# Local and global attention with a squared-ReLU MLP on one core: the jobs of the global rows, the block output copies and the weight decoding at other places of the step, and VectorE and ScalarE in program order from the first step

## The chip, the core and the metric

The kernel runs on one core of a Trainium2 chip. The metric is the device time of one execution in microseconds (us). Three runs of the kernel before gave 1134.98, 1136.09 and 1137.07 us, so the median is 1136.09 us. One more execution was profiled; it is the source of all the rows below.

In the rows, PE is TensorE's matmuls and PEld its weight loads, DVE is VectorE, ACT is ScalarE and SP is SyncE, whose queue issues every DMA of this kernel.

## The reference

Eight batches of eight heads, 512 local and 32 global positions, head dimension 64. Each local position attends to the 32 global keys and to the local keys within 32 positions; each global position attends to all 544 keys. The 4352 output rows then go through a two-layer MLP with hidden size 2048. The shape of the MLP's input is 4352 x 512.

```python
k_all = np.concatenate([k_g, k_l], axis=2)
s_g = scale * np.matmul(q_g, k_all.transpose(0, 1, 3, 2))
out_g = np.matmul(sm(s_g), v_all)
s_ll = np.where(np.abs(pos[:, None] - pos[None, :]) <= 32, scale * q_l @ k_l.T, -1e9)
a_l = sm(np.concatenate([s_lg, s_ll], axis=-1))
out_l = np.matmul(a_l, np.concatenate([v_g, v_l], axis=2))
x = np.concatenate([out_g, out_l], axis=2).transpose(0, 2, 1, 3).reshape(B * S, H * D)
h = np.maximum(x @ w_in, 0.0)
return h * h @ w_out
```

## The kernel before

**Steps.** One loop over t from 0 to 145 does everything. In step t the attention works on local head t: there are NT = 128 of them, each one head of one half batch (256 queries). In the same step the MLP works on m = t - 9: eight consecutive m are the eight slices of the hidden layer for one block of 256 rows, and there are 17 blocks, the last one made of all the global rows. So `gemm1(m)` (input times a slice of w_in, into the PSUM tile h, one buffer) and `gemm2(m-1)` (the squared slice times w_out, accumulated over eight steps into the two PSUM tiles o) are in every step from 9 on, and a step is named by its t. Work on attention has an eight step rhythm, and global work a rhythm of sixteen, one batch.

**A step's order.** For TensorE: in odd steps `av` (probabilities times values of two heads into the first half of the PSUM tile xa), then jobs, then `transposes(t-1)`, the scores of head t+1 (`begin`), `gemm1(m)`, `gemm2(m-1)`. For VectorE and ScalarE: in odd steps `x_evac` (ScalarE copies xa to x_h, VectorE then reads xa and x_h to write x_l), `pt_evac(t-1)` (each copies half of the transposed probabilities, pts), `softmax3(t)` (VectorE: add, reciprocal, two scalings), `split_head(t+2)` (ScalarE hi, VectorE lo), `softmax1(t+1)` (VectorE: mask and maximum, into st), `softmax2(t+1)` (ScalarE: two exponentials with their sums), the copies and additions of the global score rows (sg), `act1(m)` (ScalarE ReLU from h to r, VectorE r = h * r) and `act2(m)` (ScalarE gh, VectorE gl). For the first 16 heads, and for block 0 of the MLP, the matmuls are plain float32 and hi, lo, gh and gl fall away; block 0 squares on ScalarE.

**Jobs of the global rows.** Twice per batch, four heads' worth of global rows are ready. `g_soft` (VectorE maximum over 544 scores), `g_exp` (ScalarE exponential), `g_norm` (VectorE reciprocal), `g_load_v` (DMA), `g_tr` (ten transposes), `g_evac` (gp), `g_av` (ten matmuls into the second half of xa), `g_xs` (ScalarE copy of xa, gxs) and `g_x` (eight VectorE 32x32 transposes into xg) are hung on steps and on places within them: lines 598 to 612.

**Block outputs.** `evac(blk)` copies the two o tiles on ScalarE into ot tiles, which DMAs then store. It stands in the steps with m % 8 == 1, ahead of that step's `gemm2`, which starts the next block in the same o tiles.

**Weights.** 32 chunks of 512 KB each hold float64 weights. A chunk is loaded (wr), decoded by one ScalarE operation (`w_abs`, into wf) and two VectorE passes (`w_bits`, a letter b in PLAN each), and for the blocks after the first it is split into ws (a letter s: one ScalarE cast and one VectorE subtraction). PLAN[t] has four places per step, divided by commas: after `rise`, after the jobs "soft", after `act2`, and at the step's end. LOOK says how many chunks are loaded ahead of the one in decoding; `w_need` decodes what is missing at the start of a step.

**What sets the order.** A scheduler orders instructions, except where `InOrder` marks them to be kept in program order. FREE holds the first step from which VectorE, ScalarE and TensorE are so marked. The SP queue isn't marked; it issues in the order in which its rows stand, and a row waits there for its buffer: raw (a head's queries and keys) has 4, v 7, the weights 32 in all.

Of the kernel before, what the change touches and what calls it, by code (L numbers as in the profile page):

```python
# [7 lines left out]
F32 = mybir.dt.float32  # L8
# [8 lines left out]
P = 128  # L17
# [8 lines left out]
NSTEP = NBLK * 8  # L26
# [2 lines left out]
SCALE = 0.125  # L29
CHUNKS = ((0, 128), (320, 128), (128, 96), (224, 96))  # L30

PLAN = [",,,b", "b,,,b", "b,,,b", "b,,b,", "b,,b,", "b,,b,", "b,,b,", "b,b,,b", "b,b,,b", "bb,bb,bb,bb", "bb,bb,bb,bb", "bbs,bb,bbs,bbs", "bbs,bbs,bbs,bbs", "bbs,bbs,bbs,bbs", "bbs,bbs,bs,s", "ss,s,s,s", "ss,s,s,s", "s,,s,", "s,,s,", "s,,s,", "s,,s,", "s,,s,", "s,,s,"]
FREE = (17, 17, 0)
LOOK = 2
SQ = (0, 8)
WCH = 32

# [1 line left out]
def f(ap):  # L39
    return ap.bitcast(F32)  # L40
# [19 lines left out]
def attention_moe(  # L60
# [10 lines left out]
    nc = tc.nc  # L71
# [4 lines left out]
    p2 = ctx.enter_context(tc.tile_pool(name="p2", bufs=2))  # L76
# [15 lines left out]
    def w_take(n):  # L92
        w_bufs["free"] -= n

    def load_head(t):
        raw = pq.tile([P, QK], F32, tag="raw", name=f"raw{t}")
        v = pv.tile([P, VC], F32, tag="v", name=f"v{t}")
        nc.sync.dma_start(raw, qk[t])
        nc.sync.dma_start(v, vv[t])
        heads[t] = dict(raw=raw, v=v)  # L100

    load_head(0)
    con = cp.tile([P, P + 4 * WIN], F32, name="con")
    for o, e in ((0, P + 2 * WIN), (P + 2 * WIN, P + 4 * WIN)):
        nc.sync.dma_start(con[:, o:e], consts[:, o:e])
# [79 lines left out]
    def g_add(t):  # L185
        if plain(t):
            return
        for dst, src in g_parts(t):
            ve.tensor_add(dst, src[:32], dst)
# [39 lines left out]
    def transposes(t):  # L229
        pr = prob[t % 2]  # L230
        for i, (o, n) in enumerate(CHUNKS):
            for u in range(2):
                r = half(u)
                pe.transpose(pt[u][:n, 64 * i : 64 * i + 64], pr[r, o : o + n], ident[r, r])
# [7 lines left out]
    def av(t):  # L242
        pair = [heads[t], heads[t + 1]]
        for i in range(3):
            for e, hd in enumerate(pair):
                v, pts, o = hd["v"], hd["pts"], xa[half(e), :HALF]
                if i == 0:
                    pe.matmul(o, v[:96, 128:192], pts[:96, 2:4, :], start=True, stop=False, skip_group_check=True)
                else:
                    u = i - 1  # L250
                    pe.matmul(
                        o[:, P * u : P * u + P],
                        v[:, half(u)],
                        pts[:, u, :],
                        start=False,
                        stop=i == 2,
                        skip_group_check=True,
                    )

    def x_evac(t):  # L260
        g, c = t // 8, (t % 8) // 2
        x = xa[:, :HALF]
        if g == 0:
            ac.copy(xg[:, c, :], x)
        else:
            ac.copy(x_h[:, g % 2, c, :], x)
            ve.tensor_sub(x_l[:, g % 2, c, :], x, f(x_h[:, g % 2, c, :]))
        heads[t] = heads[t + 1] = None

    state = {}  # L270

    def g_load(t):

        b, grp = t // 16, (t // 4) % 2
        qr = p2.tile([P, P], F32, tag="qr", name=f"qr{t}")
        nc.sync.dma_start(qr, qg[b, grp])
        state["q", t // 4] = qr

    def g_split(t):
        if plain(t):  # L280
# [144 lines left out]
    def act2(m):  # L425
        r = moe["r"]
        if m < 8:
            moe["g", m] = (r,)
            return
        gh = p2.tile([P, 2, HALF], F32R, tag="gh", name=f"gh{m}")  # L430
        gl = p2.tile([P, 2, HALF], F32R, tag="gl", name=f"gl{m}")
        ac.copy(gh, r)
        ve.tensor_sub(gl, r, f(gh))
        moe["g", m] = (gh, gl)
# [23 lines left out]
    def evac(blk, tiles=(0, 1)):  # L458
        for i in tiles:
            ot = p2.tile([P, DM], F32, tag="ot", name=f"ot{blk}_{i}")  # L460
            ac.copy(ot, moe["o"][i])
            if blk < NGR:
                b, hf = divmod(blk, 2)
                r0 = b * 544 + 32 + hf * 256 + i * P
                nc.sync.dma_start(out[r0 : r0 + P, :], ot)
            else:
                for bb in range(4):
                    r0 = (4 * i + bb) * 544
                    nc.sync.dma_start(out[r0 : r0 + 32, :], ot[32 * bb : 32 * bb + 32, :])
# [4 lines left out]
    def w_start(i):  # L474
        while w_next["load"] < min(WCH, i + LOOK) and w_bufs["free"] >= 2:
            w_take(1)
            w_load(w_next["load"])
            w_next["load"] += 1
        if i < w_next["load"] and i not in w_ready and (i % 2 == 1 or w_bufs["free"] >= 1):
            w_ready.add(i)  # L480
            w_abs(i)
# [29 lines left out]
    def w_tick(t, place):  # L511
        if t < len(PLAN):
            for c in PLAN[t].split(",")[place]:
                {"b": w_pass, "s": w_chunk}[c]()

    def w_need(m):

        if m < 8:
            while w_next["bits"] < 8 * m + 8:
                n = w_next["bits"]  # L520
                w_pass()
                assert w_next["bits"] > n
        elif m < 16:
            while not set(range(4 * (m - 8), 4 * (m - 8) + 4)) <= whi.keys():
                n = w_next["split"]
                w_chunk()
                assert w_next["split"] > n, (m, w_next, w_bufs, sorted(w_used)[-1:])
# [6 lines left out]
    def run_jobs(t, place):  # L534
        for job, *args in jobs.pop((t, place), ()):
            job(*args)

    def begin(t):
        scores(t)
        g_scores(t)  # L540

    def rise(t):
        softmax1(t)
        softmax2(t)

    g_load(0)
    w_start(0)
    begin(0)
    rise(0)
# [2 lines left out]
    for t in range(NSTEP + LAG + 1):  # L552
        m = t - LAG
        ve.on, ac.on, pe.on = [t >= x for x in FREE]
        prev, run, live, more = 1 <= t <= NT, 0 <= m < NSTEP, t < NT, t + 1 < NT
        pair = t - 3 if t % 2 and 3 <= t <= NT + 1 else None
        if t + 4 < NT:
            load_head(t + 4)
        if t % 4 == 0 and t + 4 < NT:
            g_load(t + 4)  # L560
        if run:
            w_need(m)

        if pair is not None:
            av(pair)
            x_evac(pair)
        run_jobs(t, "av")
        run_jobs(t, "tr")
        if prev:
            transposes(t - 1)  # L570
        if more:
            begin(t + 1)
        if run:
            gemm1(m, 0)
            gemm1(m, 1)
        if prev:
            pt_evac(t - 1)
        run_jobs(t, "evac")
        if live:
            softmax3(t)  # L580
        if t + 2 < NT:
            split_head(t + 2)
        if more:
            rise(t + 1)
        if 0 < m <= NSTEP and m % 8 == 1 and m > 8:
            evac(m // 8 - 1)
        w_tick(t, 0)
        if more:
            g_copy(t + 1)
            g_add(t + 1)  # L590
        run_jobs(t, "soft")
        if t % 4 == 2 and t + 2 < NT:
            g_split(t + 2)
        w_tick(t, 1)
        if run:
            act1(m)
        run_jobs(t, "late")
        if live and t % 4 == 3 and (t // 8) % 2 == 1:
            d = t if t % 8 == 3 else t + 1
            e = d + 4 if d % 2 else d + 5  # L600
            for at, place, job in (
                (d + 1, "soft", g_soft),
                (d + 1, "soft", g_exp),
                (d + 2, "soft", g_norm),
                (d + 2, "late", g_load_v),
                (d + 3, "tr", g_tr),
                (d + 3, "evac", g_evac),
                (e, "av", g_av),
                (e, "evac", g_xs),
                (max(e, 17), "late", g_x),  # L610
            ):
                jobs.setdefault((at, place), []).append((job, t))
        if m == NSTEP:
            for i in range(2):
                gemm2(m - 1, 0, (i,))
                gemm2(m - 1, 1, (i,))
                evac(NBLK - 1, (i,))
        elif m > 0:
            gemm2(m - 1, 0)
            gemm2(m - 1, 1)  # L620
        if run:
            act2(m)
        w_tick(t, 2)
        if 0 < m <= 8:
            w_done(m - 1)
        w_tick(t, 3)
        if 8 * NGR - 2 <= m < 8 * NGR:
            cols = (slice(0, 224), slice(224, HALF))[m % 2]
            ac.copy(x_h[:, 0, :, cols], xg[:, :, cols])
            ve.tensor_sub(x_l[:, 0, :, cols], xg[:, :, cols], f(x_h[:, 0, :, cols]))  # L630
# [69 lines left out]
```

## Time and profile before

| | |
|---|---|
| median of three runs | 1136.09 us |
| the profiled execution, its own time | 1137.75 us |
| its span, first to last instruction | 1135.9 us |
| mean granted TensorE clock | 0.972 |
| VectorE busy, ScalarE busy | 669.6 us, 552.6 us |
| loaded from HBM, stored | 65.54 MB, 8.91 MB |

The busy shares of the engines and the chain of work that ended last are quoted with the prediction. The profile divides the span in 40 slices of 28.4 us. In the first two TensorE is at 5 and 8 tenths and VectorE at 5 and 8; from the seventh to the 36th TensorE is at 8 or 9 tenths, VectorE at 5 or 6 and ScalarE at 4 or 5. The granted TensorE clock is at 7 tenths of full speed in the second slice, 8 in the fourth and sixth, and 9 or more in all others. The DMA engines are busy to 8 tenths in the first three slices and to 1 or 2 tenths after.

### The profile page before, as it was taken

To read this page: it belongs to the slowest core of one execution; us is meant where nothing else is said; L and a number is where in the kernel's file an instruction comes from. 1 tells how busy PE (TensorE), PEld (TensorE's weight loads), DVE (VectorE), ACT (ScalarE), POOL (GpSimd) and SP (SyncE) were. 2 spreads that over 40 slices of the span, in tenths; PEclk is the share of its full clock that TensorE was granted. 3 is DMA by queue.
4 is the path that set the end of the run, shared out by engine and by line. 5 is a ranking of instruction groups with operands and counts; after the bars stand their busy time and mean duration, and the time that the engine had idled before them with its cause. 6 is when DMAs were issued, how large, how long until landed. Compare 5 with 4: busy or idle time off the path is not lost.

```text
span 1135.9 us, 21870 instructions
## 1 busy us (share of the span) xinstructions
PE 1052.2 (93%) x8320; PEld 878.9 (77%) x8320; DVE 669.6 (59%) x2340; ACT 552.6 (49%) x1617; POOL 0.5 (0%) x5
## 2 busy tenths in 40 slices
PE   5898799998999989998999989998999989999998
PEld 4665578877888778877888778877888778878987
DVE  5886466565666556655666656656566666663321
ACT  5786445545554445544455454545454454543222
POOL 0000000000000000000000000000000000000000
PEclk9798989999999999999999999999999999999999
DMA  8881111121211212121211212112211212101000
GB/s 267 275 298 52 32 58 48 52 62 57 61 56 40 62 53 62 59 59 48 66 42 53 62 52 62 58 53 61 57 45 56 58 53 66 43 1 43 1 20 19
DMA packets 72458, 75.88 MB, mean 67 GB/s; under 512 B 6304, under 2 KB 63776, under 8 KB 72352
## 3 DMA queue, kind: packets, MB, share of 16 engines
q1 hardware_dynamic: 72352, 74.47, 21.6%
q8 instruction: 66, 1.08, 0.4%
q14 instruction: 40, 0.33, 0.1%
HBM read 65.54 MB, written 8.91 MB: 66 GB/s over the span
## 4 chain that ended last, share of the span: by engine, by line
PE 53%; DVE 23%; ACT 14%; issue 4%; DMA 4%; SPq 0%; ACTq 0%; DVEq 0%
PE o L53 22%; PE h L53 19%; PE xa L53 6%; DVE prob L53 6%; ACT prob L53 5%; PE sb L53 3%; DVE gl L53 3%; DVE r L53 3%; ACT gh L53 2%; PE pt L53 2%; DVE st L53 2%; DVE lo L53 2%; ACT r L53 2%; ACT sg L53 2%; DMA wr<-in_w_dram 2%
## 5 line engine op out<-in xcount | busy, mean ns | idle before, releaser
L53 PE MATMUL h<-x_h,ws 128*128 128x256 f32 x2048 | 400.8, 289 | 6.1 <-DVE r L53 6.1
L53 PE MATMUL o<-ws,gh 128*128 128x512 f32 x1024 | 326.2, 400 | 25.7 <-ACT ot L53 25.7
L53 PEld LDWEIGHTS h<-x_h,ws 128*128 128x128 f32 x2048 | 327.6, 191 | 22.0 <-DVE r L53 7.5
L53 PE MATMUL h<-x_l,ws 128*128 128x256 f32 x1024 | 289.9, 283 | 0.1
L53 ACT ACTIVATE prob<-prob,st 128x224 f32<-128x224 f32 x256 | 121.3, 475 | 259.9 <-DVE st L53 259.7
L53 PEld LDWEIGHTS o<-ws,gh 128*128 128x128 f32 x1024 | 187.0, 192 | 62.2 <-ACT ot L53 29.3
L53 PE MATMUL o<-ws,gl 128*128 128x512 f32 x512 | 203.5, 398 | 0.0
L53 PEld LDWEIGHTS h<-x_l,ws 128*128 128x128 f32 x1024 | 196.1, 192 | 1.0 <-DVE x_l L53 0.4
L53 DVE TENSOR_TENSOR sg<-sb,sg 32x128 f32<-32x128 f32 (+3 forms) x280 | 60.1, 257 | 159.5 <-ACT sg L53 159.3
L53 DVE TENSOR_TENSOR r<-h,r 128x512 f32<-128x512 f32 x128 | 88.4, 691 | 104.2 <-ACT r L53 104.0
L53 DVE TENSOR_TENSOR gl<-r,gh 128x512 fp32r<-128x512 f32 x128 | 88.7, 693 | 77.3 <-ACT gh L53 76.8
L53 ACT CAST gh<-r 128x512 fp32r<-128x512 f32 x128 | 79.3, 619 | 97.5 <-DVE r L53 97.5
L53 PEld LDWEIGHTS o<-ws,gl 128*128 128x128 f32 x512 | 97.7, 191 | 22.9
L53 ACT ACTIVATE r<-h 128x512 f32<-128x512 f32 x136 | 81.3, 598 | 61.1 <-PE h L53 58.1
L53 DVE CUSTOM_DVE_ANT_0 prob<-sb,con 128x224 f32<-128x224 f32 x248 | 86.4, 386 | 9.4 <-PE sb L53 9.1
L53 DVE COPY pts<-pt 128x256 f32<-128x256 f32 x128 | 53.5, 418 | 40.5 <-PE pt L53 40.0
L53 DVE TENSOR_SCALAR prob<-prob,st 128x224 f32<-128x224 f32 x256 | 74.7, 334 | 4.2
L53 ACT COPY pts<-pt 128x256 f32<-128x256 f32 x128 | 47.5, 371 | 60.0 <-PE pt L53 59.0
L53 PEld LDWEIGHTS xa<-pts,v 128*64 128x64 f32 (+1 forms) x768 | 47.5, 141 | 35.8 <-issue 24.1
L53 PEld LDWEIGHTS pt<-con,prob 64*128 64x128 f32 (+1 forms) x1024 | 42.3, 137 | 41.5 <-issue 27.5
L53 PE MATMUL xa<-pts,v 128*64 128x128 f32 (+1 forms) x768 | 73.9, 327 | 0.2 <-ACT pts L53 0.2
L53 PE MATMUL pt<-con,prob 64*128 64x64 f32 (+1 forms) x1024 | 61.7, 242 | 8.0 <-DVE prob L53 7.9
(69 smaller groups left out, 1050.4 us busy)
## 6 DMA issues: line engine op xcount, KB each, us to landing
raw<-in_qk_dram SPq DMA_DIRECT2D x128, 176.0 KB, 2.3
wr<-in_w_dram SPq DMA_DIRECT2D x32, 512.0 KB, 5.5
v<-in_vv_dram SPq DMA_DIRECT2D x128, 96.0 KB, 1.9
gv<-in_vg_dram SPq DMA_DIRECT2D x32, 320.0 KB, 3.4
out_dram<-ot SPq DMA_DIRECT2D x32, 256.0 KB, 2.0
qr<-in_qg_dram SPq DMA_DIRECT2D x32, 64.0 KB, 2.3
out_dram<-ot SPq DMA_DIRECT2D x8, 64.0 KB, 1.7
con<-in_consts_dram SPq DMA_DIRECT2D x1, 288.0 KB, 4.3
```

Of the source, the lines that this page charges most:

```text
L53: r = method(*args, **kwargs)
```

## The change

It does six things. `evac` goes from behind `rise` to the very front of its step. `g_av` and `g_xs` go from steps 15 and 21 of a batch's sixteen to steps 16 and 20, so from odd to even ones. `g_soft`, `g_exp`, `g_norm` and `g_x` go from their places ahead of `act1` or behind it to a new place "post", behind `act2`. FREE is 0 for all three engines, so the first 17 steps are in program order on VectorE and ScalarE too. PLAN has one decoding pass in each of steps 0 to 7 (two or three before, and one in step 0), four in step 8 (three before) and eight in each of steps 9 to 14 (the same before in steps 9 to 13, where the scheduler moved them besides); the splits end two steps later. LOOK is 4. The first load of global queries stands ahead of the constants in SP's queue.

```diff
-PLAN = [",,,b", "b,,,b", "b,,,b", "b,,b,", "b,,b,", "b,,b,", "b,,b,", "b,b,,b", "b,b,,b", "bb,bb,bb,bb", "bb,bb,bb,bb", "bbs,bb,bbs,bbs", "bbs,bbs,bbs,bbs", "bbs,bbs,bbs,bbs", "bbs,bbs,bs,s", "ss,s,s,s", "ss,s,s,s", "s,,s,", "s,,s,", "s,,s,", "s,,s,", "s,,s,", "s,,s,"]
-FREE = (17, 17, 0)
-LOOK = 2
+PLAN = [",,,b", ",,,b", ",,,b", ",,,b", ",,,b", ",,,b", ",,,b", ",,,b", "b,b,b,b", "b,bb,bbb,bb", "b,bb,bbb,bb", "b,bb,bbbs,bbs", "b,bb,bbbs,bbs", "bs,bb,bbbs,bbs", "bs,bb,bbbs,bbs", "b,bb,bbss,bs", "s,s,s,", "s,,s,s", "s,,s,s", "s,,s,", "s,,s,", "s,,s,", "s,,s,", "s,,s,"]
+FREE = (0, 0, 0)
+LOOK = 4
...
     load_head(0)
+    g_load(0)
     con = cp.tile([P, P + 4 * WIN], F32, name="con")
...
-    g_load(0)
     w_start(0)
...
         if run:
             w_need(m)
 
+        if m > 8 and m % 8 == 1:
+            evac(m // 8 - 1)
         if pair is not None:
             av(pair)
...
-        if 0 < m <= NSTEP and m % 8 == 1 and m > 8:
-            evac(m // 8 - 1)
...
-            e = d + 4 if d % 2 else d + 5
+            e = d + 5 if d % 2 else d + 4
             for at, place, job in (
-                (d + 1, "soft", g_soft),
-                (d + 1, "soft", g_exp),
-                (d + 2, "soft", g_norm),
+                (d + 1, "post", g_soft),
+                (d + 1, "post", g_exp),
+                (d + 2, "post", g_norm),
                 (d + 2, "late", g_load_v),
                 (d + 3, "tr", g_tr),
                 (d + 3, "evac", g_evac),
                 (e, "av", g_av),
                 (e, "evac", g_xs),
-                (max(e, 17), "late", g_x),
+                (max(e, 17), "post", g_x),
...
         if run:
             act2(m)
+        run_jobs(t, "post")
         w_tick(t, 2)
```

Three places show the moves. The first is TensorE's queue around a `g_av` of the second batch, before the change (step 31). xa is the tile that `av` and `g_av` share, gv and gp are the values and probabilities of the global rows, pt takes the transposes.

```order
L53 MATMUL o_2_2166<-ws_1092,gl_2474 128x512
L53 MATMUL xa<-pts_2430,v_1896 64x256
L53 MATMUL xa<-pts_2534,v_1987 64x256
L53 MATMUL xa<-pts_2430,v_1896 64x128
L53 MATMUL xa<-pts_2534,v_1987 64x128
L53 MATMUL xa<-pts_2430,v_1896 64x128
L53 MATMUL xa<-pts_2534,v_1987 64x128
L53 MATMUL xa<-gv_2458,gp_2537 64x128 x10
L53 MATMUL pt_112<-con,prob_108 128x64
```

The same `g_av` in the changed kernel (step 32), on the same engine:

```order
L53 MATMUL o_2_2165<-ws_1477,gh_2580 128x512 x2
L53 MATMUL o_2_2165<-ws_1477,gl_2581 128x512
L53 MATMUL o_2_2166<-ws_1477,gh_2580 128x512 x2
L53 MATMUL o_2_2166<-ws_1477,gl_2581 128x512
L53 MATMUL xa<-gv_2456,gp_2537 64x128 x10
L53 MATMUL pt_114<-con,prob_111 128x64
```

The ten matmuls stood right behind an `av` into the same tile; now there is no `av` in their step, and they follow the step's last `gemm2`.

The second place is ScalarE's queue in steps 33 and 34, before the change: from a global exponential (sg, gst) over the block copies (ot) to the next ReLU (r).

```order
L53 ACTIVATE sg,gst_2864<-sg,gst_2864 128x544
L53 ACTIVATE r_2868<-h_2818 128x512
L53 CAST gh_2883<-r_2868 128x512
L53 COPY pts_2934<-pt_112 128x4x64
L53 CAST hi_2941<-raw_2699 128x352
L53 ACTIVATE prob_109,st_2945<-prob_109,st_2945 128x224 x2
L53 COPY ot_0_2951<-o_2_2165 128x512
L53 COPY ot_1_2954<-o_2_2166 128x512
L53 COPY sg<-sb_110 32x128
L53 COPY sg<-sb_111 32x160
L53 CAST qz_2963<-qr_2703 128x4x32
L53 ACTIVATE r_2966<-h_2909 128x512
```

The same stretch of ScalarE's queue in the changed kernel:

```order
L53 ACTIVATE r_2864<-h_2818 128x512
L53 CAST gh_2879<-r_2864 128x512
L53 ACTIVATE sg,gst_2883<-sg,gst_2883 128x544
L53 COPY ot_0_2891<-o_2_2165 128x512
L53 COPY ot_1_2894<-o_2_2166 128x512
L53 COPY pts_2940<-pt_114 128x4x64
L53 CAST hi_2947<-raw_2679 128x352
L53 ACTIVATE prob_111,st_2951<-prob_111,st_2951 128x224 x2
L53 COPY sg<-sb_112 32x128
L53 COPY sg<-sb_113 32x160
L53 CAST qz_2961<-qr_2683 128x4x32
L53 ACTIVATE r_2964<-h_2915 128x512
```

The block copies stood between the exponentials of a head and its sg copies, and now stand ahead of pts; the global exponential stood ahead of a ReLU, and now stands behind gh.

The third place is VectorE's queue at the first two heads, before the change. prob_108 and st_130 belong to head 0, prob_109 and st_154 to head 1; ISA rows are `softmax1`, and wf is weight decoding.

```order
L53 TENSOR_SCALAR st_130<-st_130 128x2
L53 ISA prob_109,st_154<-s_0_144,con 128x224
L53 ISA st_154 128x1
L53 ISA prob_109,st_154<-s_1_145,con 128x224
L53 ISA st_154 128x1
L53 TENSOR_SCALAR wf_124<-wf_124 128x512
L53 TENSOR_SCALAR st_154<-st_154 128x2
L53 SCALAR_TENSOR_TENSOR wf_124<-wr_120,wf_124 128x512
L53 TENSOR_SCALAR st_130<-st_130 128x2
L53 RECIPROCAL st_130<-st_130 128x2
L53 TENSOR_SCALAR prob_108<-prob_108,st_130 128x224 x2
```

VectorE at the same place in the changed kernel, where head 0 is prob_110 and head 1 is prob_111:

```order
L53 TENSOR_SCALAR st_134<-st_134 128x2 x2
L53 RECIPROCAL st_134<-st_134 128x2
L53 TENSOR_SCALAR prob_110<-prob_110,st_134 128x224 x2
L53 ISA prob_111,st_158<-s_0_148,con 128x224
L53 ISA st_158 128x1
L53 ISA prob_111,st_158<-s_1_149,con 128x224
L53 ISA st_158 128x1
L53 TENSOR_SCALAR st_158<-st_158 128x2
L53 TENSOR_SCALAR wf_128<-wf_128 128x512
```

`softmax1` of head 1 stood ahead of `softmax3` of head 0, and now stands behind it; this holds for every following pair of heads.

More of the change, by code (lines that the diff above doesn't have):

```diff
@@ L100, in load_head, with g_load @@
         heads[t] = dict(raw=raw, v=v)
+    state = {}
+    def g_load(t):
+        b, grp = t // 16, (t // 4) % 2
+        qr = p2.tile([P, P], F32, tag="qr", name=f"qr{t}")
+        nc.sync.dma_start(qr, qg[b, grp])
+        state["q", t // 4] = qr
     load_head(0)
+    g_load(0)
     con = cp.tile([P, P + 4 * WIN], F32, name="con")
@@ L268, in x_evac @@
         heads[t] = heads[t + 1] = None
[L270 to L277, printed above, removed]
     def g_split(t):
```

## The prediction

> **What bounds the kernel now.** I read the page's busy times first, then its chain, then TensorE's waits behind the early part, then the rhythm of the chain, and last the rows of one step.
>
> ```profile
> PE 1052.2 (93%) x8320; PEld 878.9 (77%) x8320; DVE 669.6 (59%) x2340; ACT 552.6 (49%) x1617; POOL 0.5 (0%) x5
> ...
> PE 53%; DVE 23%; ACT 14%; issue 4%; DMA 4%; SPq 0%; ACTq 0%; DVEq 0%
> ```
>
> TensorE is busy for 93%, yet only 53% of the chain is TensorE's, and 37% is VectorE's and ScalarE's, which are busy 59% and 49% of the time. So a second chain, in which these two engines wait for each other, is nearly as long as TensorE's work. TensorE's waits from 148 us to the end:
>
> ```profile
> PE xa L53 <- DVE x_l L53: 23.1, 14, 2.3
> PE o L53 <- ACT ot L53: 20.8, 13, 2.3
> PE h L53 <- DVE r L53: 5.0, 6, 0.8
> ```
>
> Two waits, once per eight steps each, make up nearly all: `g_av` waits for `x_l`, `gemm2` for the block copies. Now the rhythm, from the chain (each row is a step's `gemm1`):
>
> ```profile
> 246.28 3.07 PE h L53 x24
> ...
> 304.12 3.07 PE h L53 x24
> ...
> 311.89 3.07 PE h L53 x24
> 318.65 3.07 PE h L53 x24
> ...
> 764.93 3.22 PE h L53 x24
> ```
>
> 246.28 is step 31 and 764.93 step 95: four periods of sixteen steps, (764.93 - 246.28) / 4 = 129.66 us each. Without a wait, a step into an odd one takes 7.77 us (304.12 to 311.89), one into an even one 6.76. Eight of each are 116.2. What else TensorE has in a period is in its timeline:
>
> ```profile
> 233.56 0.46 PE L53 MATMUL pt<-con,sg 64*128 64x64 f32 x8
> ...
> 240.69 1.09 PE L53 MATMUL xa<-pts,v 96*64 96x256 f32 x12
> 244.06 1.31 PE L53 MATMUL xa<-gv,gp 128*64 128x128 f32 x20 [2.28 <-DVE x_l L53]
> ...
> 273.79 1.22 PE L53 MATMUL o<-ws,gh 128*128 128x512 f32 x2 [2.27 <-ACT ot L53]
> ```
>
> Two `g_tr` of about 0.4 (the 0.46 of 233.56 overlap their neighbours) and two `g_av` of 1.3 bring **TensorE alone** to 116.2 + 0.7 + 2.6 = 119.5 us a period. Of 129.66 it loses 10.2, partly as slow matmuls behind a wait (the pair at 273.79 takes 1.22).
>
> The other chain, in VectorE's and then ScalarE's timeline, over a plain even step:
>
> ```profile
> 253.55 0.42 DVE L53 COPY pts<-pt 128x256 f32<-128x256 f32 x1
> ...
> 258.33 0.69 DVE L53 TENSOR_TENSOR r<-h,r 128x512 f32<-128x512 f32 x1 [0.30 <-ACT r L53]
> 259.70 0.69 DVE L53 TENSOR_TENSOR gl<-r,gh 128x512 fp32r<-128x512 f32 x1 [0.68 <-ACT gh L53]
> 260.36 0.42 DVE L53 TENSOR_TENSOR x_l<-xa,x_h 128x256 fp32r<-128x256 f32 x1
> ...
> 256.16 0.48 ACT L53 ACTIVATE prob<-prob,st 128x224 f32<-128x224 f32 x1 [2.87 <-DVE st L53]
> ...
> 257.70 0.60 ACT L53 ACTIVATE r<-h 128x512 f32<-128x512 f32 x1
> ```
>
> Program order makes one line of this: from 253.55 VectorE does pts, `softmax3`, lo and `softmax1`, at 256.16 ScalarE's exponentials can start, sg follows, at 257.70 the ReLU, at 258.33 r, then gh, and gl from 259.70 to 260.3, where the next step's first row can start. That is 6.75 us in which each of the two waits only for the other, and 0.34 more in odd steps for `x_l` (260.36 to the next row). Eight pairs are 110.7, less than TensorE's 116.2 by little. The period's extras:
>
> ```profile
> 245.82 0.42 DVE L53 COPY pts<-pt 128x256 f32<-128x256 f32 x1 [1.81 <-PE pt L53]
> ...
> 251.21 1.71 DVE L53 STREAM_TRANSPOSE xg<-gxs 32x32 f32<-32x32 f32 x8
> ...
> 265.20 0.72 DVE L53 TENSOR_REDUCE gst<-sg 128x1 f32<-128x544 f32 x1
> ...
> 279.84 0.42 DVE L53 TENSOR_TENSOR x_l<-xa,x_h 128x256 fp32r<-128x256 f32 x1 [2.11 <-ACT x_h L53]
> ...
> 266.14 0.75 ACT L53 ACTIVATE sg<-sg,gst 128x544 f32<-128x544 f32 x1 [1.33 <-DVE gst L53]
> ...
> 267.01 0.60 ACT L53 ACTIVATE r<-h 128x512 f32<-128x512 f32 x1
> ...
> 273.18 1.04 ACT L53 COPY ot<-o 128x512 f32<-128x512 f32 x2
> ```
>
> Twice each: the global softmax, 2.2 (the ReLU behind it starts at 267.01; without the wait of 1.33 and the exponential with its sum it would at 264.8); `g_x`, 1.0 (1.71 less the 0.69 in which VectorE would have waited for gh); ot, 1.05. With gp and qz (2.1, an estimate) the chain is 110.7 + 4.4 + 2.0 + 2.1 + 2.1 = 121.3. Then there are **round trips**. `g_av` waits for `x_l`, and the next pts waits 1.81 for the transposes behind `g_av`. `gemm2` waits for ot, and the next `x_l` waits 2.11 for the `av` behind that `gemm2`. Two of each add 7.8: 129.1 of the 129.66. So VectorE and ScalarE set the period, and TensorE's two waits cost it by the way back.
>
> **The change part by part, steady steps.** `g_av` now follows a step without `av`: the `x_l` before it is a step old, and both legs of its round trip go, 1.8 twice. ot at the front has the time in which ScalarE now waits 2.87 for st; `gemm2` finds o free, and both ot's 1.05 and its round trip of 2.1 go. Late next is r: TensorE's `gemm1` waits for it, a wait that sends nothing back. TensorE, let go at r, is at its next `gemm1` 6.76 or 7.77 us later and at the transposes ahead of it a microsecond sooner, and the chain wants those for pts only 8.0 us behind r (6.75 + 1.28, with gl).
>
> Two things move along. ot's stores are issued some 3 us sooner in a step, into a queue and DMA engines that are busy to a tenth or two there. gxs takes a buffer of the qr tiles, and now in the steps that load a qr; the two older ones have been read by then, in steps 14 and 18, so I cost it at nothing; were it waited for, SP would hold that step's later loads for as long as gxs takes to be read, some 10 us, against four steps of 7 us by which raw is loaded ahead.
>
> The places "post" give some back. `g_x` no longer hides 0.69 of waiting: 1.6 instead of 1.0. `g_norm` had hidden in the ReLU's wait and costs 0.3. The global softmax moves out from ahead of the ReLU, but its 0.9 on ScalarE (266.14 to 267.01) now stand ahead of what VectorE wants next. In step 13 of sixteen that is x_h: counted from r's end, gl ends at 1.28, the maximum at 2.07, the exponential at 3.0, x_h at 3.4, `x_l` at 3.8, where pts could have started at 1.62. In step 18 it is two ot, pts and hi, so lo starts 4.85 behind r instead of 2.51. So 2.2 and 2.3, as much as before. New chain: 110.7 + 4.5 + 3.2 + 0.6 + 2.1 = **121.1**. I take 121.6, since the old account was 0.5 short: 8.0 saved per period. From step 24 to 128, where the heads end, there are 6.5 periods: **52 us**. Bounds: TensorE alone, 119.5, saves 10.2, or 66 us in all; if no step's surplus is absorbed by a neighbour's slack, the period is the sum of the longer engine side step by step. That is TensorE's 119.5 plus what the chain exceeds it by in steps 13 (1.7), 14 (0.4), 16 (0.3), 18 (2.6), 20 (0.3) and 22 and 26 (0.3 each), 125.4: 28 us.
>
> **The first 24 steps** have no stall that sums as simply; their landmarks:
>
> ```profile
> 12.14 0.66 ACT L53 ACTIVATE wf<-wr 128x512 f32<-128x512 f32 x1 [10.12 <-DMA wr<-in_w_dram]
> ...
> 18.64 1.98 PE L53 MATMUL xa<-pts,v 96*64 96x256 f32 x12
> ...
> 45.00 3.72 PE L53 MATMUL h<-xg,wf 128*128 128x256 f32 x16
> ...
> 71.13 3.72 PE L53 MATMUL h<-xg,wf 128*128 128x256 f32 x16
> ...
> 80.32 3.72 PE L53 MATMUL h<-xg,wf 128*128 128x256 f32 x16
> ...
> 88.80 3.72 PE L53 MATMUL h<-xg,wf 128*128 128x256 f32 x16
> ...
> 106.36 3.74 PE L53 MATMUL h<-xg,wf 128*128 128x256 f32 x16
> ...
> 123.39 0.39 PE L53 MATMUL h<-x_h,ws 128*128 128x256 f32 x1
> ...
> 148.80 0.39 PE L53 MATMUL h<-x_h,ws 128*128 128x256 f32 x1
> ...
> 138.94 2.00 DMA out_dram<-ot
> ...
> 189.66 3.07 PE h L53 x24
> ...
> 50.00:60.00 10.00, 8.85 (x31) 6.07 (x30) 8.59 (x28) 9.12 (x26) 0.00 (x0) 0.83 0.93 326
> ...
> wr<-in_w_dram SPq DMA_DIRECT2D x32, 512.0 KB, 5.5
> ```
>
> The PE rows are the `gemm1` of steps 9, 12, 13, 14, 15, 17, 19 and 24; the last two rows are a window's busy times (TensorE, weight loads, VectorE, ScalarE, GpSimd, then the clock, the DMA share and GB/s) and the chunks' loads with their time to landing.
>
> The earlier qr gains nothing: the first exponential stands behind the first decoding in both orders, which ends at 12.8. In program order the eight heads follow one another: `softmax3` and `softmax1` 1.8 (253.55 to 256.12 less pts and lo), exponentials 1.0, two hand-overs 0.3. In odd steps pts, which stands ahead of `softmax3`, waits for an `av` of 1.98 as well, 1.1 more: 7.4 for two heads. From 14.9 (12.7, and exponentials, hand-over and `softmax3`) this gives 44.5 after eight, and `gemm1` of step 9 at 48.6 instead of 45.00: **-3.6** (3.1 a head would give +1.2, 4.5 a head -10).
>
> [...]
>
> Steps 9 to 14 stay TensorE's: 9.19 us for a step into an odd one (71.13 to 80.32) and 8.48 into an even one (to 88.80), with the same eight passes a step that keep VectorE busy for 8.6 of 10 us in the window. In program order the passes behind `act1` wait for the squares, but end about as TensorE ends `gemm2`. Step 14 to 15 took 17.56 with `g_av`'s wait; it becomes 9.2, and `g_av` costs 1.3 in step 16: **+7.1**. Steps 17 to 19 took 25.4. Now step 17 has, in a row, 6.75, `g_x` 1.6, the softmax 1.7 and three splits, 12.4; step 18 the two ot with a 2.0 us store between them, as before, and three splits, 11.7; `gemm1` of step 19 comes 20.7 behind that of step 17: **+4.7**. Steps 19 to 24 took 40.9; with two splits each (1.6) the chain is 45.2, less 1 of slack: **-3.5**. Together +4.7, between -10 and +15.
>
> The sum: 1137.75 - 52 - 4.7 = 1081 for an execution like the profiled one, which took 1.7 more than the median; I predict **1079**.
>
> **The rivals.** *TensorE alone (0.13).* The chain's slack absorbs all: 66 + 7 saved, 1063. For it speaks that TensorE's granted clock falls only behind waits; against it that the chain's own sum, 121.1, is above 119.5. *No slack absorbed (0.17).* 28 + 5, 1103. For it: r comes just before `gemm1` wants it, as the 5.0 us of h waits show. *The tile is still waited for (0.06).* If `g_av`'s wait hangs on something other than that `x_l`, only ot's part goes, about 4 of the 8: 26 + 4, 1106. Against it: the profile names `x_l` in all 14 cases. *Slower: decoding in program order (0.05).* ScalarE now takes exponentials and ReLUs behind each `w_abs`, and four chunks a step must arrive in steps 9 to 15. If only one load were under way at a time, four landings of 5.5 us would make a step 22 us instead of 8.7, seven of them 93 longer: 1172. It decides from 8.1 us lost in each of these steps. Against it: four chunks are asked for ahead, and 2.4 MB a step (with raw and v) at the window's 326 GB/s take 7.4 us. SP must also not hold them long behind a raw load that waits for its buffer, which comes free with the scores four heads earlier.
>
> **How the numbers follow.** My forecast, 1068 to 1091, has 0.55; the rest, 0.04, is a loss of the early gain and more. The range takes in both bounds, 1061 to 1105. Faster by over 0.2%, about what a measurement of this kernel can tell from no change: 0.93; within: 0.02; slower: 0.05.
>
> **What the changed profile would show.** Right: waits of xa for `x_l` and of o for ot gone; a period of 121 to 122; h waits for r of 1 to 2 us a period, at steps 18 and 21; `gemm1` of step 9 near 48.6. Wrong: a period above 125, new waits of `x_l` or lo beyond 2.3, or ScalarE waiting for wr in steps 9 to 15.

## The result, and the profile after

The changed kernel takes **1084.32 us** (median of four, 1084.02 to 1084.95), the kernel before 1136.58 us (1134.98 to 1138.75) beside it. The ratio is 0.954, with a 95% interval of 0.9523 to 0.9557: 52.3 us faster.

The engines' busy times and the chain that ended last, from the page of the changed kernel:

```profile
PE 1040.7 (96%) x8320; PEld 867.6 (80%) x8320; DVE 669.5 (62%) x2340; ACT 544.3 (50%) x1617; POOL 0.5 (0%) x5
...
DVE 40%; ACT 26%; PE 24%; issue 7%; DMA 1%; SPq 0%; ACTq 0%
```

TensorE is busy for a larger share, 96% against 93%, and yet its share of the chain fell from 53% to 24%. VectorE and ScalarE now make up 66% of it. TensorE's waits from 148 us to the end of the changed kernel (waited for, us in total, times, the longest):

```profile
PE sb L53 <- DVE sg L53: 4.5, 4, 2.9
PE h L53 <- DVE r L53: 3.3, 13, 0.3
PE o L53 <- ACT ot L53: 1.4, 6, 0.2
```

The wait of xa for `x_l`, 23.1 us, is gone; that of o for ot fell from 20.8 to 1.4. The period, from the `gemm1` of steps 31 and 95 in TensorE's timeline of the changed kernel:

```profile
239.14 0.39 PE L53 MATMUL h<-x_h,ws 128*128 128x256 f32 x1
...
724.88 0.39 PE L53 MATMUL h<-x_h,ws 128*128 128x256 f32 x1
```

(724.88 - 239.14) / 4 = 121.44 us instead of 129.66. The new rhythm can be read from r, which stands in the chain of the changed kernel in each of these steps (start, duration; steps 28 to 36):

```profile
221.38 0.70 DVE r L53
230.56 0.70 DVE r L53
238.36 0.70 DVE r L53
245.44 0.70 DVE r L53
252.19 0.70 DVE r L53
261.03 0.70 DVE r L53
270.31 0.70 DVE r L53
278.10 0.70 DVE r L53
284.85 0.70 DVE r L53
```

Steps 32 and 36 show the plain even step, 6.75 (245.44 to 252.19), step 31 the plain odd one, 7.08. The step with the global softmax ahead of x_h takes 9.18 (221.38 to 230.56), 2.1 more than a plain odd one; the one with it ahead of lo takes 9.28 (261.03 to 270.31), 2.5 more than a plain even one. `g_x` makes 8.84 of 7.08 (252.19 to 261.03).

### The profile page after: what moved, and what is told of

Read it like the earlier page. It is cut to its first block, busy times and chain, and to the rows that moved or that the text cites. A ratio compares the mean times of both kernels' runs of the same rounds, so it can differ in the third digit from the quotient of the medians.

```text
span 1082.6 us, 21919 instructions
## 1 busy us (share of the span) xinstructions
PE 1040.7 (96%) x8320; PEld 867.6 (80%) x8320; DVE 669.5 (62%) x2340; ACT 544.3 (50%) x1617; POOL 0.5 (0%) x5
## 4 chain that ended last, share of the span: by engine, by line
DVE 40%; ACT 26%; PE 24%; issue 7%; DMA 1%; SPq 0%; ACTq 0%
PE h L53 11%; PE o L53 9%; DVE prob L53 9%; ACT prob L53 8%; DVE r L53 6%; DVE gl L53 6%; ACT r L53 6%; ACT gh L53 5%; ACT sg L53 5%; DVE st L53 4%; DVE lo L53 4%; DVE pts L53 3%; PE xa L53 2%; DVE xg L53 2%; DVE x_l L53 2%
## 5 line engine op out<-in xcount | busy, mean ns | idle before, releaser
L53 PEld LDWEIGHTS h<-x_h,ws 128*128 128x128 f32 x2048 | 327.2, 191 | 19.5 <-DVE r L53 6.2
L53 PE MATMUL o<-ws,gh 128*128 128x512 f32 x1024 | 321.7, 395 | 5.5 <-ACT ot L53 5.5
L53 PEld LDWEIGHTS o<-ws,gh 128*128 128x128 f32 x1024 | 184.5, 189 | 40.0 <-ACT ot L53 7.6
L53 PE MATMUL pt<-con,prob 64*128 64x64 f32 (+1 forms) x1024 | 59.1, 235 | 8.5 <-DVE prob L53 7.7
L53 DVE TENSOR_TENSOR lo<-raw,hi 128x352 fp32r<-128x352 f32 x112 | 58.1, 518 | 9.7 <-ACT hi L53 9.7
L53 ACT COPY sg<-sb 32x128 f32<-32x128 f32 (+3 forms) x312 | 56.6, 237 | 2.8
```

The costliest lines, as they stand in the source:

```text
L53: r = method(*args, **kwargs)
```

## The experiments

**Theory:** VectorE and ScalarE, in program order, set the period; in the kernel before, TensorE's two waits add the way back to it. The gain of the steady steps is those two ways back and ot's place on that line. **Rivals:** TensorE's own work sets the period, and the change only lets it run at a better clock; or TensorE's waits, with the slow matmuls behind them, are themselves the cost; or one of the two moves does everything. The first four kernels each make one part of the change alone, on the kernel before.

### The block copies alone

```diff
+        if m > 8 and m % 8 == 1:
+            evac(m // 8 - 1)
         if pair is not None:
             av(pair)
...
-        if 0 < m <= NSTEP and m % 8 == 1 and m > 8:
-            evac(m // 8 - 1)
```

> The kernel before with the block copies alone at the front of their step. Way-back theory (VectorE and ScalarE in line set the period; a wait of TensorE costs them what comes back late): per sixteen steps the two ot leave the line (1.05 each) and so do the two waits of x_l behind them (2.1 each), 6.3 x 6.5 periods = 41 us, so about 1095 us and a period of 123.4. Rival (TensorE's waits are the cost themselves): only its 20.8 us of waits for ot go, with some 8 us of slow matmuls behind them, so 1108 to 1116.

Measured: 1103.90 us, ratio 0.9725 (0.9698 to 0.9751). TensorE's waits from 148 us on in this kernel:

```profile
PE xa L53 <- DVE x_l L53: 24.4, 14, 2.3
PE h L53 <- DVE r L53: 5.0, 6, 0.8
```

The wait for ot is gone and the other stayed as it was, 24.4 in 14 times. The period is 124.75, so the copies are worth 4.9 of the 8.2, less than the 6.3 expected. The time lies between the theory's 1095 and the rival's 1108 to 1116, so it does not decide. What the theory calls the way back is in VectorE's waits from 148 us on, first in the kernel before, then in this one:

```profile
DVE pts L53 <- PE pt L53: 32.6, 14, 3.1
DVE x_l L53 <- ACT x_h L53: 21.1, 31, 2.1
```

```profile
DVE pts L53 <- PE pt L53: 26.6, 14, 2.5
DVE x_l L53 <- ACT x_h L53: 6.6, 19, 1.5
```

The two fell by 20.5 us, 3.0 in each of the 6.8 periods from 148 us to step 128; with the copies' own 2.1 that makes 5.1, near the 4.9.

### The global value products alone

```diff
-            e = d + 4 if d % 2 else d + 5
+            e = d + 5 if d % 2 else d + 4
```

> The kernel before with the global value products alone in steps 16 and 20. Way-back theory: 1.8 twice per period, 23 us, and some 7 us at step 15, so about 1106 us and a period of 126.0. Rival (TensorE's waits): 28.5 us of waits for x_l and the slow matmuls behind them, 1098 to 1108. The time tells them apart badly; the period's waits do: by the way-back theory the waits of o for ot stay as they are.

Measured: 1100.96 us, ratio 0.9699 (0.9676 to 0.9721). Here the other wait stayed:

```profile
PE o L53 <- ACT ot L53: 20.9, 13, 2.3
PE h L53 <- DVE r L53: 7.2, 6, 1.2
DVE pts L53 <- PE pt L53: 5.6, 7, 1.7
```

The period is 125.66, 4.0 less, near the expected 126.0. VectorE's wait for pt fell from 32.6 to 5.6 us, which is 4.0 in each of the 6.8 periods, as much as the period lost. The time is 5 us below what the theory expected, and within the rival's 1098 to 1108, because the first 24 steps gained 12.2, where 7 had been expected (`gemm1` of step 24 at 177.43 instead of 189.59). The rival that one move does everything falls with these two kernels.

### The places "post" alone

```diff
-                (d + 1, "soft", g_soft),
-                (d + 1, "soft", g_exp),
-                (d + 2, "soft", g_norm),
+                (d + 1, "post", g_soft),
+                (d + 1, "post", g_exp),
+                (d + 2, "post", g_norm),
...
-                (max(e, 17), "late", g_x),
+                (max(e, 17), "post", g_x),
...
             act2(m)
+        run_jobs(t, "post")
```

> The kernel before with the global softmax, its reciprocal and the transposes of the global output alone behind act2. Way-back theory: the line gets longer, by 0.6 for each transposing job, 0.3 for each reciprocal and 0.1 for each softmax, 1.9 per period, 12 us in all: about 1149 us. Rival (the softmax taken out from ahead of the ReLU shortens the line by its 2.2, twice a period): 28 us faster, 1108. Second rival (all of it lies beside TensorE's work): 1136.

Measured: 1140.03 us (ten runs, 1136.36 to 1149.51), ratio 1.0048 (1.0023 to 1.0073). A loss of 4 or 5 us, by the interval 3 to 8, where 12 had been expected; the period is 130.42, 0.8 more, and o's wait for ot grew:

```profile
PE o L53 <- ACT ot L53: 28.8, 13, 3.1
PE xa L53 <- DVE x_l L53: 24.7, 14, 2.5
```

### The early part alone

PLAN, FREE, LOOK and the first load of qr as in the change, nothing else.

> The kernel before with the table of the weight decoding, program order from the first step, four chunks ahead and the early qr, and nothing else. Theory: the first 24 steps of the changed kernel gained 2.9 us with 7 us from step 15's removed wait in them, so this part alone costs some 4 us: 1141 (1136 to 1146), with step 9's gemm1 near 45.6. Rival (program order and the table are what saves the early time, and the removed wait would have been hidden): 1130 or less.

Measured: 1148.71 us, ratio 1.0117 (1.0092 to 1.0141). This part alone **loses 12.6 us** against 1136.09, and 13.6 against the kernel before beside it (1135.14), more than twice what was expected, and at another place: `gemm1` of step 9 comes at 46.29, near the expected 45.6, and the period is 129.62, as before, but step 24 comes 7.1 later than before and step 31 11.3 later. The last 4 are worth a look, because nothing of the change is near them. TensorE's timeline of this kernel, step 26:

```profile
216.50 1.14 PE L53 MATMUL o<-ws,gh 128*128 128x512 f32 x2 [2.12 <-ACT ot L53]
...
217.87 1.06 PE L53 MATMUL o<-ws,gh 128*128 128x512 f32 x2
...
219.15 1.04 PE L53 MATMUL o<-ws,gh 128*128 128x512 f32 x2
...
220.25 0.62 PE L53 MATMUL o<-ws,gh 128*128 128x512 f32 x2
```

and the same step of the kernel before:

```profile
208.28 0.73 PE L53 MATMUL o<-ws,gh 128*128 128x512 f32 x2 [1.03 <-ACT ot L53]
...
209.08 0.62 PE L53 MATMUL o<-ws,gh 128*128 128x512 f32 x2
```

A wait longer by 1.1 us costs the step 2.7: behind it the pairs take 1.14, 1.06 and 1.04 us, and only the fourth, 3.75 us behind the first, takes 0.62; behind the wait of 1.03, where the granted clock was 1.00, they take 0.73 and then 0.62.

### The changed kernel without "post"

The diff of the places "post", the other way round, on the changed kernel.

> The changed kernel with the global softmax, reciprocal and transposing jobs back at their old places, ahead of act1 and between r and gl. Way-back theory: the line of VectorE and ScalarE is 1.9 shorter per period, 119.2, so TensorE's 119.5 and it are about even; a period of 119.6 to 120.5, 6 to 12 us less: 1072 to 1078. Rival (the new places shorten the way to the ReLU): 2.2 twice per period lost, 28 us: 1112.

Measured: 1077.60 us, ratio to the kernel before 0.9489 (0.9469 to 0.9509), 6.7 less than the changed kernel. The period is 120.67, 0.8 less. So "post" costs in place, with 6.7 us, about what it cost alone.

### Less TensorE work, with the change and without

```diff
-                mm = [(gh, wh), (gh, wl), (gl, wh)]
+                mm = [(gh, wh), (gl, wh)]
```

Both kernels leave out one of the three products of `gemm2`, a third of its matmuls, so their output isn't the reference's.

> The changed kernel without one of the three products of gemm2 (gh times the low part of the weights), which takes 4 x 0.23 = 0.92 us per step off TensorE and nothing off the others. Line theory: the period stays at 121 (the h waits of 1.7 go into it), and only the steps behind 128, where no head is left, get shorter, 17 x 0.92 = 16 us: about 1068. Rival (TensorE sets the period): 14.7 less per period, 110 us in all: 975.

> The kernel before without the same product. Line theory: the way back behind ot gets shorter by one gemm2 (0.9, twice a period), nothing else until step 128: 12 + 16 us less, about 1109. Rival (TensorE's waits and work set the time): 110 us less, 1026.

Measured, with two runs each: 1072.97 us with the change, ratio 0.9445 (0.9414 to 0.9476), and 1112.57 us without, ratio 0.9794 (0.9764 to 0.9824); the line theory had 1068 and 1109. The `gemm1` of steps 31 and 95 with the change, and the largest wait of its matmuls from 148 us on:

```profile
241.66 0.39 PE L53 MATMUL h<-x_h,ws 128*128 128x256 f32 x1
...
727.35 0.38 PE L53 MATMUL h<-x_h,ws 128*128 128x256 f32 x1
```

```profile
PE sb L53 <- DVE sg L53: 45.5, 31, 3.5
```

(727.35 - 241.66) / 4 = 121.42: with TensorE busy for 71 us less (970.1 instead of 1040.7) the period **doesn't move**. Without the change it is 128.36 against 129.66. The gain of 11.4 us with the change is in the last 15 steps, which have no attention (from `gemm1` of step 129 to that of 144 87.14 us became 75.56); at step 129 this kernel was 1.9 behind. In both kernels TensorE waits for what it no longer works: from step 31 to step 95 it is idle for 39.1 us instead of 3.5 with the change, and for 55.8 instead of 29.5 without. So the rival that TensorE sets the period falls for both kernels, and so does the one that its waits are the cost by themselves, since they grow here while the time falls.

### The global jobs in the engines' gaps

If VectorE and ScalarE set the period, then jobs that stand where these two wait anyway should cost nothing. On the changed kernel: `g_soft` behind `rise`, where ScalarE's exponentials are still to come; `g_exp` a step later ahead of `rise`, where ScalarE waits for st; `g_norm` and `g_x` back in "late", `g_x` as half a job in each of two steps.

```diff
+        run_jobs(t, "mid")
         if more:
             rise(t + 1)
+        run_jobs(t, "gap")
...
-                (d + 1, "post", g_soft),
-                (d + 1, "post", g_exp),
-                (d + 2, "post", g_norm),
+                (d + 1, "gap", g_soft),
+                (d + 2, "mid", g_exp),
+                (d + 2, "late", g_norm),
...
-                (max(e, 17), "post", g_x),
+                (max(e, 17), "late", g_x, 0),
+                (max(e, 17) + 1, "late", g_x, 1),
```

> The changed kernel with the jobs of the global rows put where one of the two engines waits: the maximum while VectorE waits for the exponentials (1.4 us free), the exponential on ScalarE ahead of a head's exponentials in the next step (2.6 us free), the reciprocal between r and gl, and the eight transposes in two lots of four between r and gl of two steps (0.7 free each). Line theory: the line falls to 110.7 + 2.1 + some 0.6 = 113.4 per period, below TensorE's 119.5, which then sets the period: 12 us less, 1072, and TensorE waits for nothing in the steady steps. Rival (TensorE's small waits of 3.3 and 1.4 us in all are what is left to gain): 1080.

Measured: **1064.81 us** (1064.5 to 1066.9), ratio to the kernel before 0.9377 (0.9357 to 0.9398), 19.5 less than the changed kernel. `gemm1` of steps 31 and 95, and TensorE's waits from 148 us on:

```profile
232.32 0.39 PE L53 MATMUL h<-x_h,ws 128*128 128x256 f32 x1
...
709.52 0.39 PE L53 MATMUL h<-x_h,ws 128*128 128x256 f32 x1
```

```profile
PE sb L53 <- DVE sg L53: 2.3, 2, 1.2
PE h L53 <- DVE r L53: 0.2, 1, 0.2
```

The period is 119.30: TensorE alone, where 119.5 had been worked out from rows of the kernel before. The 2.1 per period are 14 us. The other 6 came before step 24 (at 180.62 instead of 186.72), 4.9 of them in steps 17 to 24, which had not been expected to gain.

### What in the early part costs

The early part loses 12.6 us alone, and the prediction had nothing of that size. Four kernels tell its pieces apart: the changed kernel with all of the early part as before; with FREE alone as before; with PLAN, LOOK and the load of qr as before, in program order; and the kernel with the jobs in the gaps with all of the early part as before.

```diff
-FREE = (0, 0, 0)
+FREE = (17, 17, 0)
```

> The changed kernel with PLAN, FREE, LOOK and the first qr load as before, so evac, g_av and the places 'post' alone are changed. Theory A (the early part costs by itself what it cost alone, 12.6 us): 1084.3 - 12.6 = 1072, gemm1 of step 24 near 175 instead of 186.72, the period as after, 121.4. Rival B (alone it cost more than here, since 4.3 of its 11.3 us came in steps 26 to 31, behind a longer wait of o for ot that the changed kernel does not have): 1077 to 1080, step 24 near 180. My prediction's early sum, in which the early part itself cost 3.6, would give 1081.

> The changed kernel with FREE as before (17, 17, 0) alone: the scheduler orders VectorE and ScalarE in steps 0 to 16 again, with the new PLAN and LOOK. If program order is what the early part costs: most of e9's gain, 1074 to 1078, and gemm1 of steps 13 to 15 without the wait for sg (step 14 near 86.5). If the plan is (passes later, splits two steps later): 1083 to 1085, as after.

> The changed kernel with PLAN, LOOK and the first qr load as before, but program order from the first step. If program order is what the early part costs: within 3 us of the changed kernel, 1082 to 1087, or slower, since two or three decoding passes then stand in each of steps 1 to 8 ahead of the heads. If the plan is: most of e9's gain, 1073 to 1078, with the splits done two steps sooner and steps 19 to 24 shorter.

> The kernel with the global jobs in the engines' gaps (e8_gap, 1064.8 us), with PLAN, FREE, LOOK and the first qr load as before. Theory A: 12.6 less, 1052, with the period at 119.3 as in e8_gap. Rival B: 1057 to 1060.

Measured, with `gemm1` of four steps from the traces:

| PLAN, LOOK, qr | steps 0 to 16 | time, us | ratio (95%) | step 9 | 13 | 15 | 24 |
|---|---|---|---|---|---|---|---|
| new | program order (the changed kernel) | 1084.32 | 0.954 (0.9523 to 0.9557) | 45.62 | 77.83 | 100.25 | 186.72 |
| old | scheduler | 1072.39 | 0.9443 (0.943 to 0.9456) | 45.38 | 78.54 | 96.04 | 175.11 |
| new | scheduler | 1073.15 | 0.9455 (0.9441 to 0.947) | 43.48 | 76.78 | 94.28 | 178.57 |
| old | program order | 1088.13 | 0.9577 (0.9563 to 0.9592) | 51.99 | 85.79 | 110.10 | 191.47 |
| old, jobs in the gaps | scheduler | 1053.68 | 0.9282 (0.9269 to 0.9295) | 45.96 | 78.52 | 96.01 | 169.55 |

Theory A holds: the early part costs 11.9 us in place and 12.6 alone. **Program order is what costs**: with the old PLAN 15.7 us, with the new one 11.2. The new PLAN, with LOOK and the load of qr, makes up 3.8 of that in program order and changes nothing that can be told apart in the times under the scheduler. (The profiled execution of the third row took 1075.70, 2.6 more than its median.)

By the landmarks the changed kernel is 11.6 behind the second row at step 24: 4.0 of it came in steps 9 to 15, 2.7 in steps 15 to 19 and 4.7 in steps 19 to 24. The last part goes with PLAN, not with the order: steps 19 to 24 take 43.64 and 43.95 us with the new PLAN, and 38.90 and 39.03 with the old. The splits differ there: ScalarE's last cast of one is in step 20 of the kernel before (160.34), and at the end of step 23, three steps later, in the changed kernel (187.15). Before that the new PLAN gains: in program order its step 9 comes 6.4 sooner, and under the scheduler its step 19 comes 1.6 sooner.

Where program order costs shows in the changed kernel's timeline of steps 13 and 14 (start, duration, engine; in brackets the idle time before):

```profile
83.72 0.16 DVE L53 TENSOR_SCALAR st<-st 128x2 f32<-128x2 f32 x1
...
84.92 0.46 PE L53 MATMUL pt<-con,sg 64*128 64x64 f32 x8
...
85.55 0.48 ACT L53 ACTIVATE prob<-prob,st 128x224 f32<-128x224 f32 x1 [3.18 <-DVE st L53]
...
86.50 0.60 ACT L53 CAST ws<-wf 128x512 fp32r<-128x512 f32 x1
87.12 0.47 ACT L53 COPY sg<-sb 32x128 f32<-32x128 f32 x3
...
87.48 0.44 PE L53 MATMUL sb<-con,sg 64*128 64x64 f32 x2 [2.10 <-issue]
...
94.36 0.15 DVE L53 TENSOR_SCALAR st<-st 128x2 f32<-128x2 f32 x1
```

One turn of VectorE, from `softmax3` to `softmax3`, takes 10.64 us here (83.72 to 94.36), because eight decoding passes and three splits stand in it in order, with two waits of 1.9 together for ScalarE; TensorE's step was 8.48. The exponentials wait 3.18 for st, which stands behind passes; a split's cast and the copies of sg come behind them. The last transposes of `g_tr` write into sb, which these copies read: TensorE, ready at 85.38, starts at 87.48, while the copies run. The profile names no releaser there, so that it is the copies is read from the order of the rows. The next `gemm1` comes 11.17 behind the last, and the one after it waits again. In the kernel with FREE alone as before, the same rows:

```profile
78.40 0.62 ACT L53 COPY sg<-sb 32x128 f32<-32x128 f32 x3 [1.04 <-DVE st L53]
...
83.87 0.46 PE L53 MATMUL pt<-con,sg 64*128 64x64 f32 x8
...
84.78 2.16 ACT L53 CAST ws<-wf 128x512 fp32r<-128x512 f32 x4
85.26 3.72 PE L53 MATMUL h<-xg,wf 128*128 128x256 f32 x16
```

The scheduler took the copies of sg ahead of the exponentials, and put four of the splits' casts in a row where nothing waits for them. Its `gemm1` of steps 13 to 15 come at 76.78, 85.26 and 94.28, so 8.48 and 9.02 apart instead of 11.17 and 11.25.

The fifth row, old early part and jobs in the gaps, is the fastest, **1053.68 us** (1053.18 to 1055.47): 30.6 below the changed kernel and 82 below the kernel before. Its chain that ended last:

```profile
PE 92%; DVE 3%; ACT 2%; DMA 2%; issue 1%; SPq 0%; ACTq 0%
```

Its period is 119.30 too. What is left to gain there is TensorE's own work, and the first 24 steps.

## Why the prediction came out as it did

1079 was predicted, 1084.32 measured. Against the kernel before that is 57 and 52.

**Steady steps: right, in mechanism and in sum.** The period was predicted at 121.1 by the sum and 121.6 as taken; it is 121.44. From step 24 to step 128 the change saves 50.4 us (838.24 became 787.89), where 52 was predicted. The profile of before had the cause on its face: two waits of 2.3 us, and two engines at 59% and 49% that make up 37% of the chain.

**Its terms were less good than the sum.** The block copies were to give 1.05 + 2.1 twice, 6.3; alone they give 4.9. `g_av` was to give 1.8 twice, 3.6; it gives 4.0. Together that is 8.9, and the changed kernel without "post" shows 9.0, so the parts add up. "post" was to give back 1.9 (g_x 1.2, `g_norm` 0.6, the softmax 0.1); it gives back 0.8. So a gain too large by 1.4, one too small by 0.4 and a loss too large by 1.1 cancelled, and that the sum came out within 0.4 is partly luck. The softmax's own size was right (2.1 and 2.5 against 2.2 and 2.3). Why "post" gives back less than its rows was not taken apart. Why the copies give less can be read in the kernel before: the 2.11 of 279.84, which the prediction took for every copy, is the exception. A period later the same row is

```profile
408.74 0.42 DVE L53 TENSOR_TENSOR x_l<-xa,x_h 128x256 fp32r<-128x256 f32 x1 [0.60 <-ACT x_h L53]
```

Of the 13 waits of `x_l` behind a copy three are 2.1 (279.84, 539.26 and 798.66) and ten 0.56 to 0.60, 0.9 in the mean; behind those three copies the granted clock was 0.50 for 3 us, behind four of the others (337.27, 404.19, 663.59 and 923.00) it was 1.00. So the term of 2.1 for the copies' way back was more than a microsecond too large, twice a period; part of that is made good by pts, whose wait fell too with the copies alone (32.6 to 26.6). The other term was too small for the like reason: behind `g_av` pts waits 1.81 or 1.82 in eight cases, of which the prediction took one, and 2.7 to 3.1 in six, 2.3 in the mean.

**h waits for r: there, but short.** 1 to 2 us a period were predicted; matmuls wait 3.3 us in the whole steady stretch, about 0.5 a period. TensorE's loss, 121.44 - 119.30 = 2.1 a period, is only partly under that name: from step 31 to step 95 TensorE is idle for 3.5 us and busy for 482.3, with the jobs in the gaps for 0.0 and 477.2. So 0.9 a period is idle time and 1.3 longer busy time, which was not taken apart.

**The first 24 steps: the sum near, the steps wrong.** +4.7 was predicted and +2.9 came. By its landmarks, changed against before:

| | predicted | measured |
|---|---|---|
| step 9 | -3.6 | -0.6 |
| steps 9 to 14 | 0 | +0.4 |
| steps 14 to 17 | +7.1 | +3.6 |
| steps 17 to 19 | +4.7 | +2.3 |
| steps 19 to 24 | -3.5 | -2.9 |

Step 9 would come at 48.6, the prediction said, from 7.4 us for two heads in a row; it came at 45.62, since the eight heads took 27.0 us (`softmax3` from 14.06 to 41.03), 6.7 for two. The step that failed is "Steps 9 to 14 stay TensorE's ... the passes behind `act1` ... end about as TensorE ends `gemm2`". It took a window of steps 9 and 10, where VectorE was busy for 8.6 of 10 us, for all six; the splits that join from step 11 on were not counted, and with them a turn takes 10.64. Up to `gemm1` of step 13 the sentence holds, the changed kernel was 2.5 ahead there; step 13 lost that again, and step 14 took 11.25 instead of the 9.2 forecast. By the second row of the table above the early part costs 11.6 up to step 24, and the other parts gain 14.5. The prediction did not split its sum in this way; its landmarks lose 7.1 (3.6 and 3.5) and gain 11.8 (7.1 and 4.7). Both were too small, by 4.5 and 2.7, and so the sum came out near by luck. The mechanism of steps 19 to 24 was right: two splits each, 3.5 predicted, 2.9 measured.

**The rivals.** TensorE alone, 1063, was not reached by the change, but the jobs in the gaps have its period. "No slack absorbed", 1103, falls with the period: 121.44, where it had 125.4. The tile is not still waited for: that wait is gone. "Decoding in program order" named the part that does cost, but not its way: ScalarE waits for no weights between 45 and 110 us, and what costs is that urgent work stands behind passes that nothing waits for.

## What to carry to other kernels

Where two engines at half load stand in most of the chain, add up one turn of their hand-overs in program order and compare it with the third engine's work; a wait of the third engine then costs what the two wait for its late result (4.0 us a period for `g_av`), and a single row of such a wait may be an exception, so read several. Ask of each side job not how long it takes but which of the two engines waits at its place: the same jobs cost 2.1 us a period in one place and nothing beyond TensorE's own work in another. And when work is put in a fixed order, count all of one turn for the step with the most in it, not for an average window, and let work with no deadline stand behind what others wait for.

## What the runs showed of the hardware

Behind a wait of 1.03 us TensorE's pairs took 0.62 again after one of 0.73, while waits of 2.12 and 3.03 us were followed by pairs at 1.04 to 1.22: for 3.75 us behind the first, and for longer behind the second. The rows of the changed kernel, step 18:

```profile
133.99 1.22 PE L53 MATMUL o<-ws,gh 128*128 128x512 f32 x2 [3.03 <-ACT ot L53]
...
136.71 1.22 PE L53 MATMUL o<-ws,gh 128*128 128x512 f32 x2 [1.06 <-ACT ot L53]
...
139.43 1.05 PE L53 MATMUL o<-ws,gh 128*128 128x512 f32 x2
...
140.84 1.09 PE L53 MATMUL xa<-pts,v 96*64 96x256 f32 x12
```

A second wait, of 1.06, stands in the middle of the slow stretch, and the pairs were slow until past 139.43, 5.4 us behind the first; the `av` at 140.84 has 1.09 again, as in the kernel before (240.69). Beside the two waits, 4.1 us in sum, the step's `gemm2` took 5.8 us, where in step 26 of the kernel before, behind its one wait of 1.03, it took 3.0: 2.8 us more. The granted clock was 0.50 from 133.99 to 139.43 and 1.00 from 140.84 on.

A wait of that length was not always followed by a lower clock. From 148 us on the kernel before has 13 waits of 2.2 or 2.3 us for `x_l` and ot. At nine of them the granted clock fell to 0.50, at most 0.4 us ahead of the wait's end and at most 0.5 us behind it, and was 1.00 again 3.4 us later (273.69 to 277.10 is one such stretch); at four of the same length (244.06, 404.19, 663.59 and 923.00) it stayed at 1.00, and so it did behind every wait of 0.8 to 1.5 us. It fell nowhere else from 148 us to TensorE's last matmul. So the length of the wait alone did not decide it here, and what did was not shown.
